# Softmax row sums and reciprocals taken for two blocks at once, on 32 rows per head

## Chip, cores and metric

The kernel runs on one core of a Trainium2 chip. The metric is the device time of one execution in microseconds. A profiled execution gives the trace; its span is the time between the first and the last instruction of the program.

## The reference

Routed attention is followed by a two-layer block with an ELU between the layers. Queries and keys are each assigned to the nearest of 16 cluster centres of their head; a query sees only the keys of its own cluster. The output of the attention becomes the input x of the second part.

```python
# q, k, v: (4, 8, 768, 64), centroids: (8, 16, 64)
q_assign = argmax(q_n . c_n);  k_assign = argmax(k_n . c_n)
mask = q_assign[:, :, :, None] == k_assign[:, :, None, :]
scores = where(mask, q @ k.T / 8, -1e9)
attn = exp(scores - max);  attn = attn / (sum(attn) + 1e-9)
x = (attn @ v) laid out as (3072, 512)
h = x @ w_in                      # (3072, 2048)
g = where(h > 0, h, exp(min(h, 0)) - 1)
out = g @ w_out                   # (3072, 512)
```

## The kernel before, in words

The first part is the attention. Its work is cut into 32 blocks: 4 batches, two halves of 384 queries, and 4 pairs of heads. One block computes scores for two heads (e = 0 and 1), all 768 keys in 6 tiles of 128 keys, and 384 queries. Keys lie on the partitions, queries along the free dimension. So the sum over the keys, which the softmax needs for each query, is a sum over partitions and over the 6 tiles.

The function `slot(n)` writes out one step of the attention by hand, in the order in which each engine's queue gets it. It works on three blocks at a time:

- For block n it makes the scores: `plain` (L498) and `masked` (L511) on TensorE into a ring of three PSUM tiles, and `exponential` (L520) on ScalarE, which leaves the probabilities of the block in `p_out`.
- For block n - 1 it makes the value product: `values` (L536) on TensorE into `o_bank`, copied to its place in `xT` by ScalarE in `take_values` (L550). VectorE meanwhile adds the 6 tiles of probabilities to one: `sums_begin` (L523), queued within slot n - 1 after the fourth key tile's scores, and `sums_end` (L528, L529) in slot n. The result, `summed`, has 384 columns for each head on 128 partitions.
- For block n - 2 it divides. `row_sums` (L554) multiplies `summed` of each head by a matrix of ones, 128 x 64, on TensorE. The 64 rows of `d_bank` that come out all hold the same sums, since the value product has one row for each of the 64 dimensions of a head. `take_sums` on ScalarE makes the logarithm (L563), a copy (L564) and the exponential of the negative logarithm (L565), that is, a first reciprocal in `r_of`, with the sums in `e_of`. `divide` improves it on VectorE (L568, L569), and GpSimd multiplies `xT` by it (L572).

Between these, some slots do work for what comes later: cluster assignment of queries or keys (`similar`, L427, on TensorE into `d_bank`, then `assign` on VectorE, L440 to L453), the masks on GpSimd (L463), transposes of the next batch's keys and queries (L659 to L673), and the preparation of the second part's weights. The weights are handled by `weigh(n)`: each piece has four steps on VectorE and one on ScalarE (L320 to L350). A hand-written table, `ROOM`, gives each slot a credit, and `COST` says what a step takes off it. The credit depends on the slot's number alone, not on times.

All loads from memory are issued on SP's queue, in the order of the code: `load_v(n + 1)` (L182) waits until the value product of block n - 1 has left its buffer, `load_k` and `load_q` (L166) fetch the next batch with 128-byte runs, and `ask` (L300) fetches weights in pieces of 1 MB.

After slot 31 the last blocks are finished (L1393 to L1406). The second part begins with `unit(0, 0)`, which multiplies a 512-token group by a part of `w_in`: seven products (L748) on sums and differences of quarters, with copies on ScalarE (L791, L795, L803, L811), additions on VectorE (L804, L813), and the ELU in three steps: exponential on ScalarE and clamping on GpSimd (`elu_exp`, L761, L762), then VectorE (`elu`, L765). `finish_attention` is called within that unit after its second product, and divides the last block there. GpSimd also prepares the next unit's weights in `w_step` (L727, L729, L731). The left-over weight steps run as `fill`. Groups after the first run in `chain` (L994, L1064).

A second path, `general_path`, is taken only if the inputs do not meet the main path's assumptions (`findings` and `verdict` decide). It reloads the weights that the main path has overwritten.

Of the kernel before, what the change touches and what calls it, by code (L numbers as in the profile page):

```python
# [9 lines left out]
F32 = mybir.dt.float32  # L10
# [4 lines left out]
Act = mybir.ActivationFunctionType  # L15
Alu = mybir.AluOpType
# [3 lines left out]
P = 128  # L20
# [41 lines left out]
def main_path(ctx, tc, c, q, k, v, centroids, moe_w_in, moe_w_out, out):  # L62


    nc = tc.nc
# [5 lines left out]
    HS = S // 2  # L71
    NPR = H // 2
    KC = DM // P
    FC = DF // P
# [7 lines left out]
    const = ctx.enter_context(tc.tile_pool(name="const", bufs=1))  # L82
# [5 lines left out]
    o_bank, d_bank = (psum.tile([P, 512], F32, name=f"{n}_bank") for n in "od")  # L88
# [14 lines left out]
    w_in, w_out = c["w_in"], c["w_out"]  # L103
# [28 lines left out]
    sim = early[:, 6912:7296]  # L132
# [3 lines left out]
    probs = [p_out[:, ts(kt, 2 * HS)].rearrange("p (e n) -> p e n", e=2) for kt in range(NT)]  # L136
    probs_all = p_out
    add_to = sums_w[:, : 4 * HS]
    summed = sums_w[:, 4 * HS : 6 * HS]
    r_of = sums_w[:, 6 * HS : 7 * HS]  # L140
    e_of = sums_w[:, 7 * HS : 8 * HS]
    ex_of = sums_w[:, 8 * HS :].bitcast(U32)
# [13 lines left out]
    blocks = [(b, half, pr) for b in range(B) for half in range(2) for pr in range(NPR)]  # L156
    NB = 2 * NPR
# [53 lines left out]
    ones = const.tile([P, D], F32, name="ones")  # L211
# [8 lines left out]
    for e in range(2):  # L220
# [5 lines left out]
            op=Alu.add,  # L226
# [22 lines left out]
    for e in range(2):  # L249
        nc.vector.tensor_scalar(cen2[:, e], cen, par[:, e : e + 1], None, op0=Alu.mult)  # L250
    cT = const.tile([P, P], F32, name="cT")
    count = const.tile([P, 4 * B], F32, name="count")
    counted = 0
    r_sum = const.tile([P, len(blocks)], F32, name="r_sum")
    d_sum = const.tile([P, len(blocks)], F32, name="d_sum")
    off = const.tile([P, 1], F32, name="off")
    nc.gpsimd.memset(off, -896.0 * 2**23)

# [101 lines left out]
    half = FC // 2  # L360
# [111 lines left out]
    def clusters_k(b, half, ps):  # L472
        cols = ts(half, HS)
        similar(kT[b % 2], cols, ps)
        return lambda: assign(hot_k[b % 2][:, :, cols], ps)

    def clusters_q(b, half, ps):
        similar(qT[half], slice(0, HS), ps)

        def told():  # L480
            assign(hot_q, ps)
            later.append(lambda: mask_q(half))

        return told
# [42 lines left out]
    def sums_end():  # L527
        nc.vector.tensor_tensor(add_to, add_to, probs_all[:, 8 * HS :], op=Alu.add)  # L528
        nc.vector.tensor_tensor(  # L529
            summed, add_to[:, : 2 * HS], add_to[:, 2 * HS :], op=Alu.add  # L530
        )

    def values(n):
        for kt in range(NT):
            for e in range(2):
                nc.tensor.matmul(  # L536
                    o_bank[64 * e : 64 * e + 64, :HS],
                    lhsT=v_raw[n % 2][:, e, kt],
                    rhs=probs[kt][:, e],
                    start=(kt == 0),  # L540
                    stop=(kt == NT - 1),
                )

    def x_of(n):
        b, half, pr = blocks[n]
        at = b * S + half * HS
        return xT[:, pr, at : at + HS]

    def take_values(n):
        nc.scalar.activation(x_of(n), o_bank[:, :HS], Act.Copy, scale=-1.0)  # L550

    def row_sums(n):
        for e in range(2):
            nc.tensor.matmul(  # L554
                d_bank[64 * e : 64 * e + 64, :HS],
                lhsT=ones,
                rhs=summed[:, ts(e, HS)],
                start=True,
                stop=True,
            )  # L560

    def take_sums(n):
        nc.scalar.activation(r_of, d_bank[:, :HS], Act.Ln)  # L563
        nc.scalar.activation(e_of, d_bank[:, :HS], Act.Copy, accum_out=d_sum[:, n : n + 1])  # L564
        nc.scalar.activation(r_of, r_of, Act.Exp, scale=-1.0)  # L565

    def divide(n):
        nc.vector.tensor_tensor(e_of, e_of, r_of, op=Alu.mult)  # L568
        nc.vector.scalar_tensor_tensor(  # L569
            r_of, e_of, -2.0, r_of, op0=Alu.add, op1=Alu.mult, accum_out=r_sum[:, n : n + 1]  # L570
        )
        nc.gpsimd.tensor_tensor(x_of(n), x_of(n), r_of, op=Alu.mult)  # L572


    def turned_by_pe(to, t, n):
# [56 lines left out]
    def slot(n):  # L632
        b, at = n // NB, n % NB
        more = b + 1 < B
        if n > 1:
            row_sums(n - 2)
            take_sums(n - 2)
        if n > 0:
            values(n - 1)
        told = None  # L640
        if at == (1 if b else 3):
            told = clusters_q(b, 1, d_bank)
        elif at == 5 and more:
            told = clusters_q(b + 1, 0, d_bank)
        elif at in (6, 7) and more:
            told = clusters_k(b + 1, at - 6, d_bank)
        if n > 0:
            sums_end()
        if n > 1:
            divide(n - 2)  # L650
        if n > 0:
            take_values(n - 1)
        if told is not None:
            told()

        if n + 1 < len(blocks):
            load_v(n + 1)
        if at == 0 and b:
            nc.vector.transpose(qT_all[1], raw_q_all)  # L659
        if at == 1 and b and more:  # L660
            load_q(b + 1, 0)
        if at == 0 and more:
            load_k(b + 1, 0)
            load_k(b + 1, 1)
        elif 2 <= at < 6 and more:
            nc.vector.transpose(kT[(b + 1) % 2][at - 2], raw_k[at % 2])
            if n == 2:
                nc.vector.transpose(qT_all[1], raw_q_all)
                load_q(1, 0)
            if at < 4:  # L670
                load_k(b + 1, at)
            elif at == 4:
                nc.vector.transpose(qT_all[0], raw_q_all)  # L673
                load_q(b + 1, 1)
        weigh(n)

        for kt in range(NT):
            s = ring()
            plain(n, kt, s)
# [695 lines left out]
        )  # L1375
        nc.vector.tensor_copy(c["go"], ps[:1, :1])

    last_n = len(blocks) - 1
    slot_first()
    for n in range(1, len(blocks)):  # L1380
        slot(n)
# [7 lines left out]
        elif last_n - 4 <= n < last_n:  # L1389
            x_sum_step(0, n - last_n + 4)  # L1390
            if n > last_n - 4:
                w_step(0, 0, n - last_n + 3)
    row_sums(last_n - 1)  # L1393
    values(last_n)
    sums_end()
    for n in range(2):
        places.append((p_out[:, ts(n, 2048)].unsqueeze(1), len(pieces)))
    ask()
    take_sums(last_n - 1)
    divide(last_n - 1)  # L1400
# [53 lines left out]
def general_path(ctx, tc, c, q, k, v, moe_w_in, moe_w_out, out):  # L1454


    nc = tc.nc
    B, H, S, D = q.shape
    NC = P // H
    w_in, w_out, cen, ident = c["w_in"], c["w_out"], c["cen"], c["ident"]  # L1460
    KC, FC = w_in.shape[1], w_out.shape[1]
# [3 lines left out]
    HS = S // 2  # L1465
# [4 lines left out]
    const = ctx.enter_context(tc.tile_pool(name="g_const", bufs=1))  # L1470
# [8 lines left out]
    def bank(dtype=F32):  # L1479
# [4 lines left out]
    MS = DM // 2  # L1484
# [7 lines left out]
    half = FC * P // 2  # L1492
# [220 lines left out]
```

## Time and profile before

| | |
|---|---|
| Three runs | 909.51, 909.56, 910.57 us (median 909.56) |
| Profiled execution | 908.84 us, span 906.6 us |
| TensorE matmul / weight load | 891.2 / 687.1 us busy (98% / 76%) |
| VectorE | 725.5 us busy (80%) |
| ScalarE | 448.9 us busy (50%) |
| GpSimd | 234.7 us busy (26%) |
| Attention slots 1 to 31 | from 24.2 us to about 336 us of the span |
| Row sums L554 | 128 records, 27.7 us busy |
| L563, L564, L565 (ScalarE) | 32 of each, mean 481, 481 and 519 ns |
| L568, L569 (VectorE) | 32 of each, mean 551 and 594 ns |
| L572 (GpSimd) | 32, mean 1104 ns |

In the rows of the profile a line number stands for the instruction's place in the code, "out<-in" names its tiles, and "idle before <-releaser" tells what ended the engine's wait. PE is TensorE's matmul, PEld its weight load, DVE VectorE, ACT ScalarE, POOL GpSimd, SP the engine that issues DMAs. One fp32 matmul leaves two records in the trace. Busy matmul time is modelled, so the pitch at which matmuls start says more than the busy share.

### The profile page before, as it was taken

How to read it: one execution, taken by the hardware profiler on the slowest of the kernel's cores; microseconds unless marked ns; L12 is line 12 of the kernel's file. 1: busy time of each engine (PE TensorE's matmuls, PEld its weight loads, DVE VectorE, ACT ScalarE, POOL GpSimd, SP SyncE). 2: the span in 40 equal slices, each digit the busy share in tenths (PEclk: the TensorE clock that was granted, in tenths of full speed). 3: DMA queues.
4: the chain of work that ended last, by engine and by line, in shares of the span. 5: the costliest groups of instructions: out<-in, count | busy, mean ns of one | idle time of the engine just before them, and what ended most of it. 6: DMA issues, size and time to landing. Idle time of an engine off the chain costs nothing.

```text
span 906.6 us, 17041 instructions
## 1 busy us (share of the span) xinstructions
PE 891.2 (98%) x6473; PEld 687.1 (76%) x6473; DVE 725.5 (80%) x1063; ACT 448.9 (50%) x883; POOL 234.7 (26%) x261
## 2 busy tenths in 40 slices
PE   8999999999999999999999999999999999999997
PEld 5444444444444448899988999899989998999897
DVE  4799999999999996995389956885688568856875
ACT  6767787777777773410133225422542254225421
POOL 1022121231303426760024202420242024202300
PEclk9999999999999999999999999999999999999999
DMA  7755554364325422102598766176617661766172
GB/s 208 188 107 157 136 135 104 105 118 122 70 82 126 160 90 79 58 25 100 180 309 295 249 211 204 47 250 209 204 46 243 211 209 48 242 212 208 45 218 93
DMA packets 153208, 138.33 MB, mean 153 GB/s; under 512 B 89248, under 2 KB 106656, under 8 KB 152096
## 3 DMA queue, kind: packets, MB, share of 16 engines
q1 hardware_dynamic: 151584, 132.45, 49.2%
q0 software_dynamic: 1248, 4.20, 1.5%
q8 instruction: 53, 0.87, 0.4%
q10 hardware_dynamic: 288, 0.52, 0.2%
q14 instruction: 35, 0.29, 0.1%
HBM read 114.59 MB, written 21.50 MB: 150 GB/s over the span
## 4 chain that ended last, share of the span: by engine, by line
PE 84%; DVE 10%; POOL 2%; issue 1%; ACT 1%; DMA 1%; SPq 0%; DVEq 0%; ACTq 0%; POOLq 0%
PE bank L994 23%; PE banks L498 12%; PE o_bank L536 12%; PE bank L748 10%; PE bank L1064 8%; PE o_bank L994 4%; PE banks L511 3%; PE d_bank L554 2%; DVE kq_g L765 2%; PE d_bank L994 2%; PE o_bank L748 2%; PE o_bank L1064 1%; PE d_bank L427 1%; PE banks L577 1%; PE d_bank L1064 1%
## 5 line engine op out<-in xcount | busy, mean ns | idle before, releaser
L520 ACT ACTIVATE p_out<-banks 128x768 f32<-128x768 f32 x192 | 155.2, 812 | 26.8 <-PE banks L511 26.7
L536 PE MATMUL o_bank<-p_out,kq_g 128*64 128x384 f32 x768 | 129.3, 486 | 0.0
L762 POOL TENSOR_SCALAR kq_g<-kq_g 128x512 f32<-128x512 f32 x96 | 70.3, 743 | 156.9 <-ACT kq_g L761 156.7
L536 PEld LDWEIGHTS o_bank<-p_out,kq_g 128*64 128x64 f32 x768 | 55.1, 137 | 68.8 <-issue 62.7
L572 POOL TENSOR_TENSOR xT<-xT,sums_w 128x384 f32<-128x384 f32 x32 | 35.3, 1104 | 222.0 <-DVE sums_w L569 164.3
L523 DVE TENSOR_TENSOR sums_w<-p_out 128x1536 f32<-128x1536 f32 x32 | 57.1, 1785 | 7.5 <-ACT p_out L520 7.5
L994 PE MATMUL bank<-w_out,kq_g 128*128 128x128 f32 x512 | 62.9, 275 | 0.0
L528 DVE TENSOR_TENSOR sums_w<-sums_w,p_out 128x1536 f32<-128x1536 f32 x32 | 59.0, 1845 | 3.3 <-DVE sums_w L523 0.5
L994 PEld LDWEIGHTS bank<-w_out,kq_g 128*128 128x128 f32 x512 | 60.4, 192 | 0.3
L748 PE MATMUL bank<-xT,spare 128*128 128x256 f32 x256 | 59.4, 379 | 0.7 <-DVE bank L804 0.7
L761 ACT ACTIVATE kq_g<-bank 128x512 f32<-128x512 f32 x68 | 39.6, 602 | 40.4 <-DVE bank L1230 16.7
L765 DVE SCALAR_TENSOR_TENSOR kq_g<-kq_g,bank 128x512 f32<-128x512 f32 x68 | 45.0, 681 | 14.7 <-POOL kq_g L762 14.7
L748 PE MATMUL bank<-x_sum,w_in 128*128 128x256 f32 x224 | 53.3, 381 | 3.0 <-DVE bank L1230 1.5
L748 PEld LDWEIGHTS bank<-xT,spare 128*128 128x128 f32 x256 | 48.3, 190 | 7.4 <-issue 1.0
L748 PEld LDWEIGHTS bank<-x_sum,w_in 128*128 128x128 f32 x224 | 42.0, 190 | 10.5 <-DVE bank L1230 2.3
L1277 DVE TENSOR_TENSOR kq_g<-kq_g 128x1024 f32<-128x1024 f32 x36 | 45.3, 1265 | 1.5 <-PE bank L994 1.5
L463 POOL TENSOR_SCALAR kq_g<-w_out,big,minus 128x768 bf16<-128x768 bf16 x16 | 34.0, 2132 | 46.1 <-ACT w_out L456 46.1
L1082 POOL TENSOR_TENSOR spare<-x_sum 128x128 f32<-128x128 f32 x16 | 7.3, 455 | 148.2 <-PE bank L1064 82.5
L498 PE MATMUL banks<-x_sum,xT 64*128 64x384 f32 x192 | 39.8, 492 | 0.0
L498 PE MATMUL banks<-kq_g 64*128 64x384 f32 x192 | 39.6, 491 | 0.0
L498 PE MATMUL banks<-kq_g,xT 64*128 64x384 f32 x192 | 39.6, 491 | 0.0
L498 PE MATMUL banks<-x_sum,kq_g 64*128 64x384 f32 x192 | 39.6, 491 | 0.0
(326 smaller groups left out, 2010.1 us busy)
## 6 DMA issues: line engine op xcount, KB each, us to landing
kq_g<-in_v_dram SPq DMA_DIRECT2D x32, 384.0 KB, 3.6
sums_w<-far_s_s SPq DMA_DIRECT2D x42, 256.0 KB, 3.6
spare<-w_far SPq DMA_DIRECT2D x32, 256.0 KB, 2.9
words_w<-far_s_s SPq DMA_DIRECT2D x26, 256.0 KB, 3.2
out_dram<-p_out SPq DMA_DIRECT2D x22, 256.0 KB, 3.3
w_out<-in_q_dram SPq DMA_DIRECT2D x112, 48.0 KB, 2.5
sums_w<-far_s_q SPq DMA_DIRECT2D x21, 256.0 KB, 3.3
words_w<-far_a_s SPq DMA_DIRECT2D x20, 256.0 KB, 3.3
```

The lines of the kernel that those rows point to most:

```text
L498: nc.tensor.matmul(s[:, e, :HS], lhsT=kT[b % 2][pr][rows, ts(kt, P)], rhs=qT[half][pr][rows], start=True, stop=False,)
L520: nc.scalar.activation(probs[kt], s[:, :, :HS], Act.Exp, scale=SCALE)
L523: nc.vector.tensor_tensor(add_to, probs_all[:, : 4 * HS], probs_all[:, 4 * HS : 8 * HS], op=Alu.add)
L528: nc.vector.tensor_tensor(add_to, add_to, probs_all[:, 8 * HS :], op=Alu.add)
L536: nc.tensor.matmul(o_bank[64 * e : 64 * e + 64, :HS], lhsT=v_raw[n % 2][:, e, kt], rhs=probs[kt][:, e], start=(kt == 0), stop=(kt == NT - 1),)
L748: nc.tensor.matmul(bank[:, ts(f, QS)], lhsT=left[:, ch, ts(f, P)], rhs=right[:, ch], start=first and f == 0 and ch == 0, stop=ch == 1, ski ...
L761: nc.scalar.activation(to, as_part(bank, to), Act.Exp)
L762: nc.gpsimd.tensor_scalar(to, to, 1.0, 0.0, op0=Alu.min, op1=Alu.max)
L765: nc.vector.scalar_tensor_tensor(to, to, -1.0, as_part(bank, to), op0=Alu.add, op1=Alu.max)
L994: nc.tensor.matmul(bank[:, :P], lhsT=left[:, f], rhs=right[:, f], start=first and f == 0, stop=last and f == 3, skip_group_check=True,)
L1064: nc.tensor.matmul(bank[:, ts(f, P)], lhsT=left[:, ts(f, P)], rhs=right, start=m in ("m1", "m5") and f == 0, stop=True, skip_group_check=True,
L1277: nc.vector.tensor_tensor(b[to][:, f], b[x][:, f], b[y][:, f], op=op)
```

## The change

The row sums of two blocks, an odd one and the even one ahead of it, are made together in the odd slots. The matrix of ones is cut to 32 columns, so each head of each block takes 32 rows of `d_bank`, and four products fill the 128 rows. One `take_sums` and one `reciprocals` then serve two blocks. The result, 128 x 384, holds block n - 1 in its upper 64 rows and block n in its lower 64. Two DMAs on SP's queue copy each half so that every row appears twice, into `r_of` and `e_of`, which makes 64 rows for each head. GpSimd multiplies both blocks in the next even slot (`scale_x`). `summed` becomes two buffers, one for even and one for odd blocks. The result of `reciprocals` goes to a buffer that is free at that time (`to_spread`). The general path reloads all of `w_in` instead of a part.

```diff
-    summed = sums_w[:, 4 * HS : 6 * HS]
+    summed = [spare.rearrange("p a n -> p (a n)")[:, 2048 : 2048 + 2 * HS]]
+    summed.append(sums_w[:, 4 * HS : 6 * HS])
...
     def row_sums(n):
-        for e in range(2):
+        for at in range(0, P, 32):
+            j, e = at // 64, at // 32 % 2
             nc.tensor.matmul(
-                d_bank[64 * e : 64 * e + 64, :HS],
-                lhsT=ones,
-                rhs=summed[:, ts(e, HS)],
+                d_bank[at : at + 32, :HS],
+                lhsT=ones[:, :32],
+                rhs=summed[(n - 1 + j) % 2][:, ts(e, HS)],
                 start=True,
                 stop=True,
             )
...
-    def divide(n):
+    def reciprocals(n):
+        at = n // 2
         nc.vector.tensor_tensor(e_of, e_of, r_of, op=Alu.mult)
         nc.vector.scalar_tensor_tensor(
-            r_of, e_of, -2.0, r_of, op0=Alu.add, op1=Alu.mult, accum_out=r_sum[:, n : n + 1]
+            to_spread(n),
+            e_of,
+            -2.0,
+            r_of,
+            op0=Alu.add,
+            op1=Alu.mult,
+            accum_out=r_sum[:, at : at + 1],
         )
-        nc.gpsimd.tensor_tensor(x_of(n), x_of(n), r_of, op=Alu.mult)
+
+    def to_spread(n):
+        if n == last_n:
+            return add_to[:, :HS]
+        return sim if n < last_n - NB else x_of(last_n)
+
+    def scale_x(n, r):
+        nc.gpsimd.tensor_tensor(x_of(n), x_of(n), r, op=Alu.mult)
+
+    def spread(n):
+        r = to_spread(n)
+        for j, to in enumerate((r_of, e_of)):
+            nc.sync.dma_start(
+                to, r[64 * j : 64 * j + 64].unsqueeze(1).to_broadcast([64, 2, HS])
+            )
...
     def slot(n):
-        if n > 1:
-            row_sums(n - 2)
-            take_sums(n - 2)
+        sums_of = n - 2 if n > 1 and n % 2 else None
+        pair_done = n - 4 if n >= 4 and n % 2 == 0 else None
+        if sums_of is not None:
+            row_sums(sums_of)
+            take_sums(sums_of)
...
         if n > 0:
-            sums_end()
-        if n > 1:
-            divide(n - 2)
+            sums_end(n - 1)
+        if pair_done is not None:
+            scale_x(n - 4, r_of)
+            scale_x(n - 3, e_of)
         if n > 0:
             take_values(n - 1)
         if told is not None:
             told()
+        if sums_of is not None:
+            reciprocals(sums_of)
...
         weigh(n)
+        if sums_of is not None:
+            spread(sums_of)
...
-    row_sums(last_n - 1)
     values(last_n)
-    sums_end()
+    sums_end(last_n)
...
-    take_sums(last_n - 1)
-    divide(last_n - 1)
+    scale_x(last_n - 3, r_of)
+    scale_x(last_n - 2, e_of)
     take_values(last_n)

     def finish_attention():
         row_sums(last_n)
         take_sums(last_n)
-        divide(last_n)
+        reciprocals(last_n)
+        spread(last_n)
+        scale_x(last_n - 1, r_of)
+        scale_x(last_n, e_of)
...
-        (w_in[:, ch, half + MS * n : half + MS * n + MS], moe_w_in[ts(ch, P), half + MS * n : half + MS * n + MS])
-        for ch in range(KC // 2)
-        for n in range(half // MS)
+        (w_in[:, ch, ts(n, MS)], moe_w_in[ts(ch, P), ts(n, MS)])
+        for ch in range(KC)
+        for n in range(FC * P // MS)
```

More of the change, by code (lines that the diff above doesn't have):

```diff
@@ L251, in main_path @@
     cT = const.tile([P, P], F32, name="cT")
+    last_n = len(blocks) - 1
     count = const.tile([P, 4 * B], F32, name="count")
     counted = 0
-    r_sum = const.tile([P, len(blocks)], F32, name="r_sum")
-    d_sum = const.tile([P, len(blocks)], F32, name="d_sum")
+    r_sum = const.tile([P, len(blocks) // 2], F32, name="r_sum")
+    d_sum = const.tile([P, len(blocks) // 2], F32, name="d_sum")
     off = const.tile([P, 1], F32, name="off")
@@ L525, in sums_begin, with sums_end @@
         )
-    def sums_end():
+    def sums_end(n):
         nc.vector.tensor_tensor(add_to, add_to, probs_all[:, 8 * HS :], op=Alu.add)
         nc.vector.tensor_tensor(
-            summed, add_to[:, : 2 * HS], add_to[:, 2 * HS :], op=Alu.add
+            summed[n % 2], add_to[:, : 2 * HS], add_to[:, 2 * HS :], op=Alu.add
         )
@@ L562, in take_sums @@
     def take_sums(n):
+        at = n // 2
         nc.scalar.activation(r_of, d_bank[:, :HS], Act.Ln)
-        nc.scalar.activation(e_of, d_bank[:, :HS], Act.Copy, accum_out=d_sum[:, n : n + 1])
+        nc.scalar.activation(e_of, d_bank[:, :HS], Act.Copy, accum_out=d_sum[:, at : at + 1])
         nc.scalar.activation(r_of, r_of, Act.Exp, scale=-1.0)
-    def divide(n):
+    def reciprocals(n):
+        at = n // 2
         nc.vector.tensor_tensor(e_of, e_of, r_of, op=Alu.mult)
         nc.vector.scalar_tensor_tensor(
-            r_of, e_of, -2.0, r_of, op0=Alu.add, op1=Alu.mult, accum_out=r_sum[:, n : n + 1]
-        )
-        nc.gpsimd.tensor_tensor(x_of(n), x_of(n), r_of, op=Alu.mult)
+            to_spread(n),
[5 more added lines that the diff above has]
+            accum_out=r_sum[:, at : at + 1],
+        )
+    def to_spread(n):
[10 more added lines that the diff above has]
+            )
     def turned_by_pe(to, t, n):
@@ L1376, in verdict @@
         nc.vector.tensor_copy(c["go"], ps[:1, :1])
-    last_n = len(blocks) - 1
     slot_first()
@@ L1491, in general_path @@
     ]
-    half = FC * P // 2
     again += [
-        (w_in[:, ch, half + MS * n : half + MS * n + MS], moe_w_in[ts(ch, P), half + MS * n : half + MS * n + MS])
-        for ch in range(KC // 2)
-        for n in range(half // MS)
+        (w_in[:, ch, ts(n, MS)], moe_w_in[ts(ch, P), ts(n, MS)])
+        for ch in range(KC)
+        for n in range(FC * P // MS)
     ]
```

## The prediction

> **What bounds the kernel now.** I read the utilisation slices of the page first, then the busy times of single slots, then TensorE's own timeline, then the waits. A slot is told here as the stretch from its first value product (L536) to the next slot's.
>
> ```profile
> PE   8999999999999999999999999999999999999997
> DVE  4799999999999996995389956885688568856875
> ACT  6767787777777773410133225422542254225421
> ```
>
> The change acts in slices 2 to 16, the attention stage. TensorE and VectorE are both full there, so the page alone doesn't say which sets the pace. The windows do, here slot 4 (no cluster work) and slot 5 (with cluster work):
>
> ```profile
> core 0: us, PE busy (x) PEld busy (x) DVE busy (x) ACT busy (x) POOL busy (x), PEclk, DMA share, GB/s
> 54.15:63.86 9.71, 9.71 (x66) 4.61 (x64) 9.47 (x10) 7.74 (x14) 4.86 (x3) 1.00 0.83 163
> 63.86:74.36 10.50, 10.50 (x75) 4.76 (x73) 10.08 (x15) 6.72 (x12) 1.00 (x1) 1.00 0.42 67
> ```
>
> TensorE fills both without a gap, and from slot 2 on every slot of the first kind lasts 9.71 us, every one of the second kind 10.50, whatever VectorE has in it (one slot apart, below). Such a pitch is TensorE's. VectorE runs behind it: its first sum (L523) starts 0.03 to 4.2 us after the exponentials that it reads, and ends at least 1.55 us before the next block's exponentials need the buffer. So TensorE sets the pace and VectorE has a small reserve. Now the price of the row sums, from TensorE's timeline:
>
> ```profile
> 23.86 0.39 PE L511 MATMUL banks<-kq_g,w_out 64*128 64x384 bf16 x2
> 24.18 0.54 PE L536 MATMUL o_bank<-p_out,kq_g 128*64 128x384 f32 x2
> ...
> 62.91 0.33 PE L511 MATMUL banks<-kq_g,w_out 64*128 64x384 bf16 x2
> 63.16 0.87 PE L554 MATMUL d_bank<-sums_w,ones 128*64 128x384 f32 x4
> 63.86 4.04 PE L536 MATMUL o_bank<-p_out,kq_g 128*64 128x384 f32 x24
> 67.83 0.85 PE L427 MATMUL d_bank<-x_sum,cT 128*32 128x384 f32 x8
> ```
>
> Slot 1 has no row sums: from the last score to the first value product 0.32 us. Slot 5 has them: 0.95. By starts, 63.16 to 63.86, they take 0.70; by the difference 0.63, but the scores before slot 1 ran 0.06 slow (0.39 against 0.33). I take 0.69. L427 is four products onto 32 rows each, the form that the new row sums have; it makes a slot 10.50 - 9.71 = 0.79 us longer.
>
> **What the Trainium skill says.** "TensorEngine Tiling (Array Packing)", Key Properties: matmuls on different column tiles run side by side, and a change of the tiling mode drains the array. The trace agrees: the 8 records of L427 take little over what 4 records on 64 columns take (0.79 against 0.69 us); that the extra 0.10 is the switch to another mode is my reading. "DMA: Bandwidth & Descriptors", Anatomy of one DMA, puts a fixed cost of about 2 us on a small transfer (a fit for the other queue), and says that waits are served by the issuing sequencer, so a waiting issue holds what stands behind it. Here 256 KB transfers out of SBUF from SP's queue landed in 2.0 to 4.3 us, median 2.1. "GPSIMD Engine Reference", Specifications: GpSimd shares SBUF interfaces with VectorE. Here the same L727 took 2.29 us beside VectorE's L340 and 1.28 us later.
>
> **Part by part.** *Row sums in the loop.* Before, slots 2 to 31 have one each: 30 x 0.69 = 20.7 us. After, odd slots 3 to 31: 15 x 0.79 = 11.9 us. TensorE gains 8.8 us. Bounds of the new form: 0.69, if the mode switch hides, gives 10.3; 0.95 gives 6.5.
>
> *Row sums at the end.* Before, one ahead of values(31) and one after the second product: 1.38. After, one of 0.79: gain 0.6.
>
> *ScalarE and VectorE.* Three passes of ScalarE (0.48 + 0.48 + 0.52) and two of VectorE (0.55 + 0.59) go from each even slot; nothing off TensorE's path counts for itself. But per pair VectorE is relieved by 1.14 us and TensorE by 2 x 0.69 - 0.79 = 0.59, so VectorE's delay shrinks and TensorE stays the bound. One stall hangs on that delay: in slot 23
>
> ```profile
> 251.44 0.85 PE L427 MATMUL d_bank<-kq_g,cT 128*32 128x384 f32 x8 [0.90 <-ACT sums_w L564]
> ```
>
> ScalarE came late there, since L330 ahead of it waited for L328 of a late VectorE. With up to 0.55 us per pair regained since slot 5, this goes: gain 0.9 (bounds 0 and 0.98).
>
> *The two transfers.* 196 KB each, 1.5 KB rows, SP's queue. They come last in an odd slot's SP order and wait for VectorE's reciprocals. Behind them stands the next slot's value load, which waits anyway until some 4 us into that slot for the value products, and lands in 3.6 us for use a slot later: nothing. Landing: 2.1 us like the SBUF transfers, up to 8 behind others. The readers are GpSimd's multiplies (1.00 us each, two in an even slot), then ScalarE's L563 in the next odd slot, which rewrites the same buffers 0.3 us into it and may come 2.3 us later before its pass over the values is late. From VectorE's reciprocals to there is over one slot, 9 to 12 us; landing and multiplies need 4 to 6. It holds in most slots. In slots 9 and 17 the 16 query loads (11.5 us of issuing) stand ahead of the transfers; there they may land 8 us into the next slot or later, at a cost of 0 to 1 us. I put 0 and keep 2 as the end.
>
> *Multiplies.* Same number, 32, moved to even slots in pairs, also behind the mask work (2 x 2.2 us) in slots 2, 6, 10 and so on; GpSimd is idle most of a slot: nothing.
>
> *The end.* Here the transfer is not hidden. These are GpSimd's and VectorE's rows:
>
> ```profile
> 348.08 1.00 POOL L572 TENSOR_TENSOR xT<-xT,sums_w 128x384 f32<-128x384 f32 x1 [4.59 <-DVE sums_w L569]
> 349.05 2.29 POOL L727 TENSOR_TENSOR spare<-w_in 128x512 f32<-128x512 f32 x1
> 352.41 0.62 POOL L762 TENSOR_SCALAR kq_g<-kq_g 128x512 f32<-128x512 f32 x1
> ...
> 353.06 0.69 DVE L765 SCALAR_TENSOR_TENSOR kq_g<-kq_g,bank 128x512 f32<-128x512 f32 x1 [2.90 <-POOL kq_g L762]
> 362.99 0.69 DVE L804 TENSOR_TENSOR o_bank<-o_bank,spare 128x512 f32<-128x512 f32 x1
> 363.82 1.97 PE L748 MATMUL o_bank<-xT,spare 128*128 128x256 f32 x8 [0.66 <-DVE o_bank L804]
> ```
>
> After the reciprocals (347.86) come 0.2 for SP, 2.1 to 2.4 of landing, and two multiplies of 1.0: L727 starts near 352.3 instead of 349.05, 3.25 later. VectorE is done with L340 by then, so L727 takes 1.28 instead of 2.29. L762 and L765 come 2.25 later. From L765 to L804 VectorE runs without a gap over 0.1 us, and TensorE waits 0.66 for L804 already: all 2.25 reach TensorE, and the second product behind is TensorE's again. Cost 2.25; ends 1.0 (some of it taken back by VectorE without GpSimd beside it) and 4.5 (landing of 4.3).
>
> *The other path* (reload of all of w_in) is not executed: no row of it is in the trace.
>
> **Sum:** -8.8 - 0.6 - 0.9 + 2.25 = -8.05. The profiled execution takes 908.84 us (span 906.6, 2.2 around it): 900.8. The median of the runs is 909.56, 0.72 above it; measured from there 901.5, which I predict.
>
> **Rivals.** *A: gain kept, but the end costs its upper bound and slots 9 and 17 lose 2 in all*: -8.05 + 2.25 + 2 = -3.8: 905.8. For: the 4.3 us maximum and SP's queue; against: the query loads are over by then. *B, slower: ScalarE is held by late transfers.* L563 can't rewrite the buffers until both multiplies have read them. Past 2.6 us into the odd slot each further us goes to TensorE, 15 times; from 8.05 / 15 = 0.54 us of it, 3.1 us into the odd slot, the change loses. If every pair landed as late as I fear for slot 17 (multiplies done 3.8 us in, 1.2 too late), it is 15 x 1.2 = 18 us: 919.5. For: one queue holds loads, weights and these; against: most weight loads are issued in even slots, ahead of the slot without transfers. *C: VectorE is the bound after all*, since GpSimd's paired multiplies stretch it (L529 takes 1.55 instead of 0.96 beside GpSimd), or the new form drains more: half of TensorE's gain goes, 4.4: 905.9. *D: it doesn't pay at all*: the 32-row products run one after another, 4 x 0.64 = 2.6 instead of 0.79 (0.64 is four passing records at 0.16): 15 x 1.8 = 27 us slower. L427 excludes it, as its slots show.
>
> **How the numbers follow.** Forecast 0.65; A 0.10; C 0.08; same 0.05 (between C and B); B 0.12; D under 0.01. The forecast's own range: low from 0.69 per new row sum (-1.5), the end at 1.0 (-1.25) and slot 23 at 0.98: 898.5; high with 4.5 at the end: 904. With A and C the range is 898 to 907. A measurement can tell about 0.2% (1.8 us) from no change: faster 0.82, same 0.05, slower 0.13.
>
> **What would show it.** Since the row sums of slot n + 1 lie at the end of stretch n, even stretches of 9.81 us (10.60 with cluster work) and odd ones of 9.02 (9.81); no wait of L427 in slot 23; VectorE waiting for exponentials more often; landing of the transfers near 2.1 us; L727 some 3 us later after the last reciprocals, and TensorE's wait for L804 near 2.9 us. It is wrong if L563 waits for GpSimd's multiplies, if stretches exceed 11 us, or if VectorE's L523 moves later.

## The result, and the profile after

After the change the kernel takes 913.02 us (median of 10 runs, 911.47 to 915.68), against 909.53 us for the kernel before beside it (10 runs, 909.04 to 911.54). The ratio is 1.0037, with a 95% interval of 1.0027 to 1.0047: slower by 3.5 us. I had predicted 901.5 us, with a range of 898 to 907. The profiled execution of after took 911.47 us, with a span of 909.7 us against 906.6 before. It was the fastest of the ten, 1.5 us under their median, so the rows below may show a mild case.

The line numbers have moved in after: the scores are L500 and L513, the exponentials L522, the value product L538, the cluster assignment L429 and L442 to L455, the row sums L558, ScalarE's three passes L568 to L570, the reciprocals L574 and L575, GpSimd's multiply L592, the two transfers L597.

The slices of the page look as before. TensorE is as full, and ScalarE and VectorE have a little less to do in slices 3 to 16:

```profile
PE   8999999999999999999999999999999999999996
DVE  4789999898999995995389956885688568856784
ACT  6667766676667763410133225422542254225421
```

The loss is seen only stretch by stretch. Below, the first two rows are slots 4 and 5, the same two as before the change. Then come slots 14, 15, 19 and 29, each again from its first value product to the next slot's. Columns: start and end of the stretch, its length, then busy time and records for each engine, the granted clock (PEclk), and the busy share and rate of the DMA engines.

```profile
core 0: us, PE busy (x) PEld busy (x) DVE busy (x) ACT busy (x) POOL busy (x), PEclk, DMA share, GB/s
53.65:63.49 9.84, 9.84 (x70) 4.46 (x68) 9.70 (x7) 7.03 (x11) 5.03 (x4) 1.00 0.94 200
63.49:73.34 9.85, 9.85 (x72) 4.48 (x68) 9.43 (x13) 6.22 (x11) 1.48 (x1) 1.00 0.41 66
153.06:166.11 13.05, 10.93 (x78) 4.63 (x76) 9.98 (x9) 7.23 (x11) 7.63 (x4) 0.98 0.71 187
166.11:177.37 11.26, 11.26 (x73) 4.94 (x69) 10.88 (x18) 7.85 (x13) 0.00 (x0) 0.87 0.12 35
206.92:217.89 10.97, 9.34 (x65) 4.26 (x61) 8.81 (x10) 6.59 (x12) 2.82 (x2) 1.00 0.72 181
307.05:316.11 9.06, 9.06 (x64) 4.31 (x60) 8.89 (x8) 5.99 (x11) 2.67 (x3) 1.00 0.67 219
```

The reader is to see two things. Slots 4, 5 and 29 behave as forecast: 9.84 and 9.85 us with TensorE busy throughout (forecast 9.81 for both, an even slot without and an odd one with cluster work), and 9.06 for an odd slot without it (forecast 9.02). Slots 14, 15 and 19 don't: in 14 TensorE is busy for 10.93 of 13.05 us, in 19 for 9.34 of 10.97. In 15 it is busy throughout, at a mean clock of 0.87.

The table sums each profile up in three stages: the attention loop from the start of slot 1 to the value product of the last block; the second part, from the first product of `unit(0, 0)` (L748 before, L782 after) to the last product of the program; and what follows the last product to the end of the span.

| us | loop | second part | after the last product |
|---|---|---|---|
| before | 312.26 | 559.45 | 6.3 |
| after | 310.77 | 562.36 | 7.85 |

So the loop gained 1.5 us where 10.4 were forecast (8.8, the 0.69 of the row sums behind slot 31, and 0.9 of slot 23), and the second part, with the division of the last blocks in it, lost 2.9 (forecast 2.25 and 0.1 of row sums). The rest, 1.55 us, lies behind the last product.

**What holds slot 14.** First SP's queue, then VectorE's row at the assignment, then TensorE. "[2.83 <-DMA ...]" is the engine's idle time before the row, and what ended it.

```profile
143.57 10.64 SPq L167 DMA_DIRECT2D w_out<-in_q_dram  x16
154.32 0.56 SPq L183 DMA_DIRECT2D kq_g<-in_v_dram  x1
154.98 1.40 SPq L302 DMA_DIRECT2D w_out<-in_moe_w_in_dram  x1
156.47 1.23 SPq L597 DMA_DIRECT2D sums_w<-w_out  x2
...
164.46 0.58 DVE L442 STREAM_TRANSPOSE w_out<-d_bank 128x384 f32<-128x384 f32 x1 [2.83 <-DMA sums_w<-w_out]
...
165.09 0.52 PE L558 MATMUL d_bank<-spare,ones 128*32 128x384 f32 x2 [2.12 <-DVE w_out L442]
```

The two transfers (L597) of slot 13 are issued at 156.5 us, 3.4 us into slot 14, behind 16 query loads, a value load and a 1 MB piece of weights. They land at 163.8 and 164.3, 7.3 and 7.2 us after their issue. Their source is `sim`, in the tile `w_out`, where `to_spread` puts the reciprocals. The assignment in slot 14 writes that same place in its first instruction (L442), so VectorE stands for 2.83 us. The row sums write `d_bank`, which L442 reads, so TensorE stands for 2.12 us.

**What holds slot 19.** The transfers of slot 17 are issued at 203.7, again behind 16 query loads and a 1 MB piece, and land at 210.2 and 210.8, 3.3 and 3.9 us into slot 19:

```profile
210.28 2.82 POOL L592 TENSOR_TENSOR xT<-xT,sums_w 128x384 f32<-128x384 f32 x2 [6.12 <-DMA sums_w<-w_out]
...
211.47 0.49 ACT L568 ACTIVATE sums_w<-d_bank 128x384 f32<-128x384 f32 x1 [3.18 <-POOL xT L592]
...
213.14 0.49 ACT L569 ACTIVATE sums_w<-d_bank 128x384 f32<-128x384 f32 x1 [1.17 <-POOL xT L592]
...
215.26 0.59 PE L500 MATMUL banks<-x_sum,xT 64*128 64x384 f32 x2 [1.63 <-ACT p_out L522]
```

This is the wait of rival B, down to the instruction: the logarithm (L568, L563 before) can't rewrite its buffer until GpSimd's multiply has read it, ScalarE's exponentials behind it come late, and TensorE's scores wait for them.

**What holds the end.** GpSimd's, VectorE's and TensorE's rows after the last reciprocals, which answer to the last lines of before:

```profile
346.65 1.17 SPq L597 DMA_DIRECT2D sums_w<-sums_w  x2
...
349.56 1.96 POOL L592 TENSOR_TENSOR xT<-xT,sums_w 128x384 f32<-128x384 f32 x2 [7.59 <-DMA sums_w<-sums_w]
351.47 1.27 POOL L761 TENSOR_TENSOR spare<-w_in 128x512 f32<-128x512 f32 x1
...
354.48 0.69 DVE L799 SCALAR_TENSOR_TENSOR kq_g<-kq_g,bank 128x512 f32<-128x512 f32 x1 [6.16 <-POOL kq_g L796]
...
364.59 0.69 DVE L838 TENSOR_TENSOR o_bank<-o_bank,spare 128x512 f32<-128x512 f32 x1
...
365.42 1.97 PE L782 MATMUL o_bank<-xT,spare 128*128 128x256 f32 x8 [2.96 <-DVE o_bank L838]
```

Here the chain ran as forecast: the transfers, two multiplies, the weight step (1.27 us instead of 2.29, forecast 1.28), and TensorE waiting 2.96 us for L838 (forecast near 2.9).

### The profile page after: what moved, and what is told of

Its sections match the earlier page's. It is cut to its first block, busy times and chain, and to the rows that moved or that the text cites. A ratio compares the mean times of both kernels' runs of the same rounds, so it can differ in the third digit from the quotient of the medians.

```text
span 909.7 us, 17041 instructions
## 1 busy us (share of the span) xinstructions
PE 886.3 (97%) x6473; PEld 681.3 (75%) x6473; DVE 717.2 (79%) x1015; ACT 426.2 (47%) x819; POOL 247.2 (27%) x261
## 4 chain that ended last, share of the span: by engine, by line
PE 77%; DVE 11%; DMA 4%; SPq 2%; issue 2%; ACT 2%; POOL 1%; DVEq 0%; ACTq 0%; POOLq 0%
PE bank L1028 23%; PE bank L782 11%; PE o_bank L538 10%; PE banks L500 9%; PE bank L1098 8%; PE o_bank L1028 4%; DVE kq_g L799 2%; PE d_bank L1028 2%; PE banks L513 2%; PE o_bank L782 2%; SPq L167 2%; DMA sums_w<-w_out 2%; PE o_bank L1098 1%; PE d_bank L429 1%; PE d_bank L558 1%
## 5 line engine op out<-in xcount | busy, mean ns | idle before, releaser
L522 ACT ACTIVATE p_out<-banks 128x768 f32<-128x768 f32 x192 | 153.4, 812 | 27.8 <-PE banks L513 26.0
L538 PE MATMUL o_bank<-p_out,kq_g 128*64 128x384 f32 x768 | 132.3, 494 | 0.5 <-DMA kq_g<-in_v_dram 0.5
L538 PEld LDWEIGHTS o_bank<-p_out,kq_g 128*64 128x64 f32 x768 | 52.7, 138 | 76.6 <-issue 71.8
L592 POOL TENSOR_TENSOR xT<-xT,sums_w 128x384 f32<-128x384 f32 x32 | 48.0, 1539 | 134.0 <-DMA sums_w<-w_out 92.8
L525 DVE TENSOR_TENSOR sums_w<-p_out 128x1536 f32<-128x1536 f32 x32 | 58.3, 1821 | 7.5 <-ACT p_out L522 7.4
L530 DVE TENSOR_TENSOR sums_w<-sums_w,p_out 128x1536 f32<-128x1536 f32 x32 | 61.2, 1913 | 2.9
L782 PE MATMUL bank<-xT,spare 128*128 128x256 f32 x256 | 59.4, 379 | 0.6 <-DVE bank L838 0.6
L782 PE MATMUL bank<-x_sum,w_in 128*128 128x256 f32 x224 | 53.3, 381 | 3.0 <-DVE d_bank L1264 1.5
L782 PEld LDWEIGHTS bank<-xT,spare 128*128 128x128 f32 x256 | 48.3, 190 | 7.4 <-issue 1.0
L782 PEld LDWEIGHTS bank<-x_sum,w_in 128*128 128x128 f32 x224 | 42.0, 190 | 10.5 <-DVE d_bank L1264 2.3
L500 PE MATMUL banks<-x_sum,xT 64*128 64x384 f32 x192 | 39.9, 493 | 1.6 <-ACT p_out L522 1.6
L500 PE MATMUL banks<-x_sum,kq_g 64*128 64x384 f32 x192 | 39.7, 492 | 0.1
L500 PE MATMUL banks<-kq_g 64*128 64x384 f32 x192 | 39.6, 491 | 0.0
L500 PE MATMUL banks<-kq_g,xT 64*128 64x384 f32 x192 | 39.6, 491 | 0.0
```

The costliest lines, as they stand in the source:

```text
L500: nc.tensor.matmul(s[:, e, :HS], lhsT=kT[b % 2][pr][rows, ts(kt, P)], rhs=qT[half][pr][rows], start=True, stop=False,)
L525: nc.vector.tensor_tensor(add_to, probs_all[:, : 4 * HS], probs_all[:, 4 * HS : 8 * HS], op=Alu.add)
L538: nc.tensor.matmul(o_bank[64 * e : 64 * e + 64, :HS], lhsT=v_raw[n % 2][:, e, kt], rhs=probs[kt][:, e], start=(kt == 0), stop=(kt == NT - 1),)
L592: nc.gpsimd.tensor_tensor(x_of(n), x_of(n), r, op=Alu.mult)
L782: nc.tensor.matmul(bank[:, ts(f, QS)], lhsT=left[:, ch, ts(f, P)], rhs=right[:, ch], start=first and f == 0 and ch == 0, stop=ch == 1, ski ...
```

## The experiments

My theory after this: the four-product row sums bring what they should, and the loss comes from where the two transfers stand in SP's queue, with the buffer that they read and the division of the last blocks as further terms. The main rival: the paired multiplies and the new rhythm on VectorE and ScalarE cost as much, whatever the transfers do. A second rival: the longer reload list of the path that isn't taken costs something. All ratios are to the kernel before, run on the same chip, with the 95% interval.

**e7_issue_early: the transfers at the earliest place on the same queue.**

```diff
         if sums_of is not None:
             reciprocals(sums_of)
+            spread(sums_of)
...
         weigh(n)
-        if sums_of is not None:
-            spread(sums_of)
```

> The changed kernel with the loop's transfers still on SP's queue, but issued directly behind the reciprocals in the order of the code: ahead of the odd slot's value load, query loads and 1 MB weight piece instead of behind them. Theory (what stands ahead in the same queue makes them land late): landing falls to about 3 us in every slot, stalls of slots 14, 15 and 19 go, 906 us beside a kernel before at 908.7. Rival (SP now waits for VectorE's reciprocals, 8 to 9 us into the slot, with the value load behind it): the value products wait for their load instead and the time stays at 911 to 913.

Measured: 907.15 us against 909.46, ratio 0.9974 (0.9965 to 0.9984). The loop takes 307.16 us instead of 310.77. SP's queue in the slot that stood in after:

```profile
143.17 10.58 SPq L167 DMA_DIRECT2D w_out<-in_q_dram  x16
153.86 1.22 SPq L597 DMA_DIRECT2D sums_w<-w_out  x2
155.18 1.23 SPq L183 DMA_DIRECT2D kq_g<-in_v_dram  x1
156.51 0.44 SPq L302 DMA_DIRECT2D w_out<-in_moe_w_in_dram  x1
```

The transfers are issued 2.6 us earlier, ahead of the 1 MB piece, and land at 157.6 and 158.1 instead of 163.8 and 164.3. In slot 17 they are issued at 192.9 instead of 203.7, ahead of the query loads, and land after 2.8 and 2.9 us. The stalls of slots 14, 15 and 19 are gone. Nothing else was changed, so the order on SP's queue is shown to be worth 3.6 us of the loop, net. By the ratios (1.0037 and 0.9974) it is 5.7 us.

The rival came true in part as well. TensorE now waits for value loads and, in slots 21 and 23, for ScalarE:

```profile
PE d_bank L429 <- ACT sums_w L569: 2.0, 2, 1.5
PE o_bank L538 <- DMA kq_g<-in_v_dram: 1.7, 3, 0.7
```

(Columns: us in total, how often, the longest.) By the lengths of the slots, the value loads cost 0.6 us in slot 2, as in after, then 0.8 in slot 12, 0.2 in slot 19 and 0.5 in slot 27, 2.1 in all. The load that slot 12 waits for is issued at 134.6 us, behind the transfers, against 128.4 in after. The other two land about as late as in after (212.1 and 293.5 us, against 212.1 and 294.7), but TensorE now gets there sooner. Not every transfer lands early either: six still take 6.1 to 7.2 us, in slots 5, 11 and 27.

**e2_act_queue: the transfers of the loop from ScalarE's queue**, after the last exponential of the odd slot (the two at the end stay on SP).

```diff
-    def spread(n):
+    def spread(n, by=None):
+        by = by or nc.sync
...
-            nc.sync.dma_start(
+            by.dma_start(
...
         weigh(n)
-        if sums_of is not None:
-            spread(sums_of)
...
+        if sums_of is not None:
+            spread(sums_of, nc.scalar)
         flush()
```

> The changed kernel with the two transfers of the loop issued from ScalarE's queue, behind the last exponential of the odd slot, instead of SP's; the last pair stays on SP. Theory (place in the queue): they no longer stand behind 1 MB weight pieces and query loads, land in about 3 us instead of up to 7.3, and the stalls of slots 14 (2.4 us), 15 (1.4, half clock) and 19 (1.9) go: 907.3 us. Rival (the paired multiplies and the smaller products are what costs, wherever the copies are issued): 913 us or more, as ScalarE also gets two issues of some 0.6 us in each odd slot.

Measured: 912.28 us against 908.74, ratio 1.0037 (1.0024 to 1.0051); loop 309.49. The stalls of slots 14, 15 and 19 are gone here too, and another one takes their place in slot 6. SP's queue and its wait in this stretch (us in total, how often, the longest), then TensorE's row:

```profile
61.57 17.09 SPq L167 DMA_DIRECT2D w_out<-in_q_dram  x16
78.76 0.56 SPq L302 DMA_DIRECT2D words_w<-in_moe_w_in_dram  x1
79.42 0.89 SPq L183 DMA_DIRECT2D kq_g<-in_v_dram  x2
...
SPq L167 <- DMA sums_w<-w_out: 5.8, 1, 5.8
...
86.30 0.87 PE L538 MATMUL o_bank<-p_out,kq_g 128*64 128x384 f32 x4 [2.48 <-DMA kq_g<-in_v_dram]
```

The 16 query loads took 17.09 us instead of 11.47 in after, the value load behind them came late, and the value product waited 2.48 us for it. The 5.8 us between the twelfth and the thirteenth load are a wait for a transfer of the other queue: ScalarE issued it at 73.31 us, it landed at 76.06, and SP issued its next load at 76.08. In the trace this transfer and that load signal their landing on the same semaphore, which ties the two queues together; why the program gave them the same one wasn't looked into. The same wait, 5.7 us, stands in this slot of e6. L429 also waited 0.72 and 1.46 us for ScalarE. The other queue took the transfers out of SP's order, but one of them still landed only 8.1 us after its issue (slot 13). The Trainium skill, "DMA: Bandwidth & Descriptors", Issuing engines are not separate DMA queues, states that transfers issued from different engines run on the same 16 DMA engines and interleave. The 8.1 us landing fits that. So a second queue was no cure in itself.

**e3_own_place: a source that no assignment rewrites.** The reciprocals of the early slots go to a place in `xT` that is filled only later.

```diff
     def to_spread(n):
         if n == last_n:
             return add_to[:, :HS]
+        if n < 3 * NB - 4:
+            return x_of(3 * NB - 1)
         return sim if n < last_n - NB else x_of(last_n)
```

> The changed kernel with the reciprocals of blocks 1 to 19 written to the place of a later block's x instead of the cluster assignment's scratch (sim); the transfers stay on SP. Theory (two causes): VectorE's assignment no longer waits for a transfer that reads sim, so slot 14's 2.4 us and the half clock behind it (1.4) go, and slot 19's 1.9, which is ScalarE waiting for the multiplies, stays: 909.2 us. Rival (landing time alone): the stall only moves to the next reader, 912 to 913 us.

Measured: 910.46 us against 908.74, ratio 1.0021 (1.0012 to 1.0031); loop 309.30. L442 no longer waits, but the transfers of slot 13 now land 8.9 and 8.8 us after their issue, and the next in line waits for them:

```profile
170.17 0.49 ACT L569 ACTIVATE sums_w<-d_bank 128x384 f32<-128x384 f32 x1 [1.83 <-POOL xT L594]
...
170.81 0.53 PE L429 MATMUL d_bank<-xT,cT 128*32 128x384 f32 x4 [1.67 <-ACT sums_w L569]
```

So another source alone moves the wait from the writer of the source to the next writer of the target. Slots 14 and 15 lose 1.7 us together, against 3.8 in after, while slot 19 still loses 1.8. The buffer decided who waited here, and the place in the queue how late the transfers came.

**e4_end_as_before: the last two blocks divided each by its own sums on 64 rows, without transfers**, as the kernel before does it.

```diff
+    def divide_one(n, at):
+        for e in range(2):
+            nc.tensor.matmul(
+                d_bank[64 * e : 64 * e + 64, :HS],
...
+            lambda: scale_x(n, r_end),
+        ]
...
+    first = divide_one(last_n - 1, last_n // 2)
     values(last_n)
...
     def finish_attention():
-        row_sums(last_n)
-        take_sums(last_n)
-        reciprocals(last_n)
-        spread(last_n)
-        scale_x(last_n - 1, r_of)
-        scale_x(last_n, e_of)
+        for step in divide_one(last_n, last_n // 2 + 1):
+            step()
```

> The changed kernel with the last two blocks divided as before, each by its own row sums on 64 rows and with no transfer, into a free buffer. Theory: GpSimd gets to its first weight step 3 us earlier, TensorE's wait for L838 falls from 2.96 us to about 0.7: 910.0 us. Rival: VectorE is full in that stretch whatever GpSimd does, so the time stays near 913.

Measured: 908.09 us against 908.74, ratio 0.9994 (0.9986 to 1.0001). The second part takes 559.08 us, against 562.36 in after and 559.45 before, and TensorE waits less for the same addition:

```profile
365.66 0.67 PE L813 MATMUL o_bank<-xT,spare 128*128 128x256 f32 x2 [0.64 <-DVE o_bank L869]
```

This shows the end's share: the transfer there costs 3.3 us of this stage, of which the row sums of block 30 take back 0.7 in slot 31, where they now stand: net 2.6. By the ratios (1.0037 and 0.9994) it is 0.0043 of 909, 3.9 us. The profiled execution was one of the slowest of its kernel, 910.12 us: its stall in slot 14 was longer than that of after, though nothing was changed there, and its loop took 314.08 us.

**e5_no_copies: all 32 transfers left out**, so GpSimd multiplies by what stands in the buffers (both calls of `spread` removed).

> The changed kernel without any of the 32 transfers: GpSimd multiplies by what ScalarE left in the two buffers, so x is scaled by numbers that are not spread over the rows. All else stays (paired row sums on 32 rows, VectorE's and ScalarE's passes, the multiplies in even slots). Theory (the transfers eat the gain): stalls of slots 14, 15 and 19 and most of TensorE's 2.96 us wait at the end go; against a kernel before at 908.7 us some 903 us (ratio 0.993 to 0.994). Rival (paired multiplies beside VectorE and the mode switch cost it): 910 us or more.

Measured: 905.24 us against 909.46, ratio 0.9956 (0.9943 to 0.9969). The loop takes 307.35 us, the second part 559.64. So with no transfer at all the loop is no better than with early ones (e7: 307.16), though in part for other reasons. The largest idle times of TensorE that are left in the loop, by what ended them:

```profile
PE banks L500 <- ACT p_out L522: 2.0, 2, 1.2
...
PE d_bank L429 <- ACT sums_w L569: 1.4, 1, 1.4
```

(Columns as under e7.) They wait for ScalarE, not for a transfer. By the lengths of the slots, 1.1 us are lost in slot 16, 1.4 in 23 and 1.4 in 28. The main rival is thus true in part: some 4 us of the loop's forecast gain (worked out below) are lost without any transfer. Slot 23 loses 1.5 in e7 and e8 too (1.0 before), so its stall needs no transfer at all; slots 16 and 28 stall by 0.2 at most there.

**e6_all, e8_early_place_end, e10_early_end: combinations.** e6 is e2, e3 and e4 together, e8 is e7, e3 and e4 together, both with the short list of e1; e10 is e7 and e4 alone. Their diffs are those shown.

> ScalarE's queue for the loop's transfers, the own place for the reciprocals, the end as before, and the shorter list of the path not taken, together. The single edits gave 0.0 (queue), -1.5 (place), -3.9 (end) and -0.3 us (list). If they add, 906.5 us beside a kernel before at 908.7. If the stalls stand in for each other (one late transfer stops one engine or the next), place and queue together give more than their sum: 903 us.

> As the run with the early issue on SP's queue, and also the own place for the reciprocals, the end as before and the shorter list of the path not taken. Theory: no stall of the loop is left but the value load of slot 2 and the end costs nothing, so the row sums' 7.6 us show nearly whole: 901 to 902 us beside a kernel before at 908.7. Rival (value loads late behind SP's wait): 907 or more.

> The changed kernel with the early issue on SP's queue and the end as before, but the reciprocals still in the assignment's scratch and the longer list kept. It tells whether the place still matters once the transfers land early. If late landing was the one cause, it takes as long as the run with all (ratio 0.994); if the place is a cause of its own, 1.5 us more (0.996).

| | this / before, us | ratio (95%) | loop | second part |
|---|---|---|---|---|
| e6 | 907.11 / 909.46 | 0.9974 (0.9966 to 0.9983) | 309.41 | 559.08 |
| e8 | 903.54 / 909.46 | 0.9942 (0.9929 to 0.9955) | 307.03 | 559.09 |
| e10 | 904.53 / 909.22 | 0.9947 (0.9934 to 0.9961) | 307.65 | 559.08 |

e8 and e10 beat both kernels: by some 5 us the kernel before, by some 9 the change as it was made. Their intervals overlap, so the place of the reciprocals isn't shown to matter once the transfers are early. By its ratio against e7's (0.9974) e10 shows the old end to be worth 2.5 us. e6 shares e3's place and e4's end with e8, and its loop is 2.4 us longer: early on SP is better than late on ScalarE's queue. Slot 6 alone, with the wait described under e2, makes up 2.5 us.

**e1_general_back and e9_before_long_list: the list of the path that isn't taken.** e1 is after with the short list, e9 is before with the long one:

```diff
     again += [
-        (w_in[:, ch, ts(n, MS)], moe_w_in[ts(ch, P), ts(n, MS)])
-        for ch in range(KC)
-        for n in range(FC * P // MS)
+        (w_in[:, ch, half + MS * n : half + MS * n + MS], moe_w_in[ts(ch, P), half + MS * n : half + MS * n + MS])
+        for ch in range(KC // 2)
+        for n in range(half // MS)
     ]
```

> The changed kernel (median 913.0 us) with one part undone: the reload list of the path that is not taken is the shorter one of before. Theory: the 1.4 us by which VectorE's last semaphore instruction comes late after the last product (909.37 where the other engines have theirs at 907.9) belongs to the longer code that is jumped over; it goes, 911.6 us. Rival: that wait is chance, or belongs to the transfers: 913.0 and the late instruction is still there.

> The kernel before with one part of the change alone: the longer reload list in the path that is not taken. Theory (the jump over longer code delays an engine at the very end): 1.4 us more, ratio 1.0015. Rival (the late last instruction is chance, as four profiles gave 6.0 to 8.0 us after the last product): 1.0000 within 0.0008.

Measured: e1 911.88 us against 908.74, ratio 1.0034 (1.0024 to 1.0045); e9 908.79 against 909.22, ratio 0.9994 (0.9986 to 1.0002). The second rival falls: taking the list back from after changes nothing that can be told, and putting it into before doesn't either. The time behind the last product, 7.85 us in after, was 6.04 in e1 and 5.69 in e9, but 8.04, 7.36 and 7.05 in e2, e3 and e10, which differ in nothing that runs there. So I count it as varying from execution to execution; what makes it vary stays open.

## Why the prediction was wrong

The sum of the prediction against the two profiles, span against span (us, negative is a gain):

| term | predicted | measured |
|---|---|---|
| row sums, loop and end | -8.8 - 0.6 | -8.1 |
| slot 23's stall | -0.9 | -0.45 |
| other stalls in the loop | 0 | +7.3 |
| the end | +2.25 | +2.8 |
| behind the last product, and the start of slot 1 | 0 | +1.6 |
| sum | -8.05 | +3.1 |

**The step that failed is "The two transfers"**, where it says "It holds in most slots" and "I put 0 and keep 2 as the end". The measured stalls of the loop, from the lengths of the slots, are 0.62 us in slot 2, 0.09, 0.42 and 0.41 in slots 6, 8 and 10, 2.43 in 14, 1.41 in 15, and 1.90 in 19, together 7.3. Of these, 14, 15 and 19 (5.7) are gone when the transfers are issued early (e7). The net gain of that is 3.6, since other stalls grew there: in slots 12, 19 and 27, where TensorE waited for value loads, and in 21 and 23, where it waited for ScalarE. What caused the stalls of slots 6, 8 and 10 was not followed up. Four things went wrong in the step:

- *What stands ahead of the transfers.* I named the query loads of slots 9 and 17 and argued that "most weight loads are issued in even slots". In after, the transfers of slots 5, 13, 15, 17 and 23 have a 1 MB piece just ahead of them (in slot 5 with a value load between), and those of slots 5, 9, 13, 17 and 21 the 16 query loads (10.6 to 11.7 us of issuing). The prediction did not go through SP's order slot by slot.
- *The landing.* Predicted 2.1 us, from 256 KB transfers out of SBUF. Measured for these:

```profile
DMA to landing us min/median/max: 2.8/2.9/7.3
```

  Twelve of the 32 took over 4 us, among them all with a 1 MB piece just ahead. The Trainium skill, "DMA: Bandwidth & Descriptors", Queues, rings and completion order, states that each DMA engine takes the descriptors of one queue in ring order; the trace agrees, 7.3 us behind the piece in slot 13 of after and 3.7 ahead of it in e7.
- *Who waits.* I named GpSimd's multiplies and L563. The source of the transfers has a next writer as well: the assignment's transpose, which stood for 2.83 us and held the row sums, and through them TensorE. I did not ask which instruction next writes what the added transfer reads.
- *The clock.* After slot 14's stall TensorE ran at half clock for 3.41 us, from 165.58 us on. The 2.9 us of it that fall into slot 15 cost half of that, about its 1.41. In the windows (same columns as above) PEclk goes from 0.93 in the stall to 0.50 and back:

```profile
163.00:166.00 3.00, 0.91 (x8) 0.16 (x8) 1.48 (x3) 0.83 (x2) 1.95 (x2) 0.93 0.38 113
166.00:168.00 2.00, 2.00 (x10) 0.77 (x8) 1.97 (x6) 1.02 (x2) 0.00 (x0) 0.50 0.00 0
170.00:172.00 2.00, 2.00 (x18) 0.58 (x14) 1.90 (x2) 0.83 (x3) 0.00 (x0) 1.00 0.00 0
```

  Over the whole execution the granted clock was 0.992 to 0.997 in the ten of after, and 0.998 to 1.0 in the 31 of before that stand beside e1 to e4.

**Row sums: right, a little small.** Without them an odd slot lasts 9.066 us; before it lasted 9.712, so two products on 64 rows cost 0.646 (I took 0.69). The even slot lasts 9.849, so the four on 32 rows cost 0.783 (0.79 taken). A pair saves 0.51 instead of 0.59. Rivals C's drain and D's serial products did not come. The loop without any stall would take 312.26 - (31 x 0.646 - 15 x 0.783) - 0.97 = 303.0 us, 0.97 being slot 23's stall of before. e7, e8 and e5 reach 307.0 to 307.4, but that they agree is chance. Of the 4.2 us of e7, 2.1 are waits for value loads and 2.1 for ScalarE (slots 21 and 23). Of the 4.4 of e5, 0.2 is a value load and the rest stalls without any transfer. Of the 4.0 of e8, 0.7 are the row sums of block 30, which that kernel has in the loop, and 0.6 is a value load.

**VectorE's reserve: wrong.** *ScalarE and VectorE* forecast 1.14 us less work for VectorE per pair, 17 us over the 15 pairs of the loop, and that its delay would shrink. In the loop VectorE was busy for 298.0 us before, 289.5 in after, 291.0 in e7 and 292.3 in e5. So it was relieved of 6 to 8.5 us, about as much as TensorE, whose row sums in the loop fell by 8.3. What is missing went into longer passes. So *Multiplies: nothing* is in doubt too. With both in one slot GpSimd's multiply took longer than the 1104 ns of before:

```profile
L592 POOL TENSOR_TENSOR xT<-xT,sums_w 128x384 f32<-128x384 f32 x32 | 48.0, 1539 | 134.0 <-DMA sums_w<-w_out 92.8
```

They stretch with VectorE's two-input additions beside them, and VectorE's additions with them: L523 took 1785 ns on average before and 1821 after, L528 1845 and 1913 (L525 and L530). L529 (now L531) took 1369 ns in the even slots, which have the multiplies, and 996 in the odd ones; its output goes to another tile in each. The mean of GpSimd's multiplies was 1.5 us in e5 too, so the transfers are not what stretched them. The stalls behind ScalarE fit that, as rival C had it, but no run took the pairing alone away: that it causes them is argued, not shown.

**Slot 23: wrong.** I let its stall go because VectorE would be ahead. It is 0.45 us in after, but 1.5 in e7 and 1.45 in e8:

```profile
245.30 1.15 ACT L332 ACTIVATE sums_w<-sums_w,off 128x1024 uint32<-128x1024 uint32 x1 [1.28 <-DVE sums_w L330]
...
247.35 0.85 PE L429 MATMUL d_bank<-kq_g,cT 128*32 128x384 f32 x8 [1.45 <-ACT sums_w L600]
```

ScalarE's weight step still waits for VectorE's. My reading is that the less TensorE stalls ahead of this slot, the later VectorE is against it.

**The end: mechanism right, size small.** Predicted +2.25, measured 2.9 between the two profiles' second parts with the row sums' 0.14 in it, and 3.3 with e4, or 2.6 net of the row sums that e4 moves into the loop. The term that was too small is the landing, 2.8 instead of 2.1 us; the upper end of 4.5 holds it.

**Rivals.** B, at 0.12, was the nearest: its mechanism came, but in single slots (14, 19), not in every pair, and it was joined by the wait on the source. Its "1.2 too late" in slot 17 was 1.9. A slower end and 5.7 us of such stalls already outweigh the 8.1 of the row sums.

## What to carry to other kernels

A small transfer that work waits for is priced by what stands ahead of it in its queue, in the slot where it is issued: list that order slot by slot, and put the issue directly behind the instruction that makes its source, ahead of bulk loads. Then look at the loads that now stand behind it and wait for the same instruction: in e7 that cost 0.8 us in slot 12. For each added transfer ask who next writes its source, not only who reads its target. At the end of a stage, where no other work covers a transfer, do without it: the old form on the last two blocks was worth 2.5 us with early transfers in the loop (e7 to e10), and 2.6 to 3.9 with late ones (e4).

## What the runs showed of the hardware beyond that

- Idle stretches of TensorE of 2.0 to 3.5 us were followed by half clock in 6 of 10 cases over all profiles, for 3.41 us each and once for 6.83 us (e4); kernels without such a stretch (before, e5, e8, e9, e10) showed none before the end. The Trainium skill, "TensorE: Matmul & The Clock Gate", Part 1, gives about 3.4 us of idling as the limit. Here 2.12 us were enough in slot 14 of after, so a stall can cost more than its own length.
- GpSimd's multiply of 128 x 384 took 0.99 us alone and up to 3.01 us beside VectorE's additions. In the end, without those, two took 1.96.
- The issue of 16 query loads on SP took 10.6 to 11.7 us in after, but 17.0 in its first batch, which stands behind three 1 MB pieces (17.1 in before). In e2 the batch of slot 5 took 17.1, with 5.8 us of it spent waiting for a transfer that ScalarE had issued.
- In the loop VectorE's L531 and GpSimd's multiplies slowed each other: L531 took at most 0.96 us while GpSimd was idle, and up to 1.64 beside it.
